# Issuing the V loads of batches 2 to 7 from GpSimd in place of the ACT queue

## The chip, the core and the metric

The kernel runs on one core of a Trainium2 chip. Its engines are TensorE (PE, matmuls), VectorE (DVE), ScalarE (ACT), GpSimd (POOL) and SyncE (SP, which here only issues transfers); 16 DMA engines move data between HBM and the on-chip memory. The metric is the device time of one execution in microseconds (us). The kernel before takes 307.86 us, the median of 3 runs (307.82 to 308.49).

## What is computed

Sliding-window causal attention over 8 batches, 8 heads, 576 positions and head size 64, followed by a two-layer network with a hard-swish:

```python
scores = (q @ k.transpose(0, 1, 3, 2)) / sqrt(64)          # 8 x 8 x 576 x 576
rel = pos[:, None] - pos[None, :]
scores = where((rel >= 0) & (rel < 64), scores, -1e9)       # window of 64
attn = softmax(scores)
x = (attn @ v).transpose(0, 2, 1, 3).reshape(4608, 512)
h = x @ w_in                                                # 512 -> 2048
y = (h * clip(h + 3, 0, 6) / 6) @ w_out                     # 2048 -> 512
```

All inputs and the output are float32 in HBM; the kernel casts to bfloat16 on chip.

## The kernel before

The program is laid out by a planner: the Python code keeps a model of when each engine is free (`pl.op(engine, ready, duration, function)`) and emits the instructions of each engine in the order that this model gives. The durations in it are only for that order; the chip runs each engine's list in order, with semaphores between engines.

Work goes in blocks of 512 rows. In block T, TensorE does the first layer (`s1`, line 812), then the second layer (`s2`, line 860), and between the matmuls of the second layer it does the scores and the PV product of batch T+1. From batch 2 on, a batch comes in through these steps:

- Q and K are loaded by SP into float32 staging tiles, cast by GpSimd into `nat`, and turned by two DMA transposes on SP (`QKT<-nat`).
- V is loaded in five pieces (four of 128 positions and a tail of 64) and cast by GpSimd twice, into `V` and, shifted by 64 positions, into `W` (which lives in a buffer that the profile names `runs`).
- Scores on TensorE (line 672), exponentials on ACT (678), mask on VectorE (683), PV on TensorE (699), division on VectorE (740), and a DMA transpose on SP into `xT`, which the next block's first layer reads.

The streaming of V, which the change touches:

```python
def stream_v(b):
    V, W = V_ring[b % 2], W_ring[b % 2]
    tiles = {}
    deps = stage_slot([...]) + (("pv", b - 2, NG - 1), ("issued", b, 1 if b == NR6 else 0))   # NR6 = 2
    tdeps = tail_slot([("cast", b, 2, KB - 1)])
    def issue(kb):                                   # kb = 0 .. 4, piece 4 is the tail
        ss = min(P, S - kb * P)
        def fn(s):
            # ... (staging tiles are taken at kb == 0)
            st = tiles["l"][:ss, :] if kb == KB - 1 else tiles["t"][:, kb, :]
            nc.scalar.dma_start(
                out=st.rearrange("p (h d) -> p h d", h=H),
                in_=v[b, :, kb * P : kb * P + ss, :].rearrange("h s d -> s h d"),
            )
            # ... (the planner's guess of when it lands)
            sv = st.rearrange("p (g h d) -> p g h d", g=NG, h=2)
            todo = [(("POOL",), W[D:P, :, kb, :, 0:D], sv[0:D], H * D)]
            if ss == P:
                todo.append((("POOL",), V[:, :, kb, :, 0:D], sv, H * D))
                todo.append((("POOL",), W[0:D, :, kb + 1, :, 0:D], sv[D:P], H * D))
            casts(("cast", b, 2, kb), land, todo)
            if kb < KB - 1:
                pl.op("ACT", s + (VGAP2 if b == NR6 else VGAP), 0.45, issue(kb + 1))   # VGAP = VGAP2 = 1.8
        return fn
    pl.op("ACT", 0.0, 0.45, issue(0), deps=deps + tdeps)
```

What waits for V: all five pieces of a batch must be cast before its first PV product.

```python
def pv(b, g):
    for r in soft(b, g) + vcasts(b, g):      # the masks, and the casts of all 5 pieces of V
        pl.wait(r)
    # ... matmuls of line 699, then reciprocal and multiplication on DVE
    def xdma(t):                              # the transpose into xT, issued by SP
        ...
        nc.sync.dma_start_transpose(out=xT[...], in_=cell["o"][...])
```

In a block the side work is placed at fixed matmuls of the second layer:

```python
REST = ((11, "S", 0), (18, "S", 1), (25, "PV", 0), (25, "PV", 1), (35, "PV", 2), (35, "PV", 3))
```

Of the kernel before, what the change touches and what calls it, by code (L numbers as in the profile page):

```python
# [24 lines left out]
VGAP = 1.8  # L25
VGAP2 = 1.8
# [79 lines left out]
def kernel(  # L106
# [9 lines left out]
    nc = tc.nc  # L116
# [19 lines left out]
    NR6 = 2  # L136
# [3 lines left out]
    pl = Plan()  # L140
# [123 lines left out]
    def stage_slot(casts):  # L264

        stage_hist.append(casts)
        return tuple(stage_hist[-1 - NSTAGE]) if len(stage_hist) > NSTAGE else ()
# [37 lines left out]
    def casts(key, land, pieces):  # L305

        left = [len(pieces)]
        def one(t):
            left[0] -= 1
            if not left[0]:  # L310
                pl.mark(key, t)
        for eng, o_ap, i_ap, cols in pieces:
            copy_op("cast", eng, cols, land, o_ap, i_ap, None, one)
# [3 lines left out]
    def tail_slot(casts):  # L317
        tail_hist.append(casts)
        return tuple(tail_hist[-4]) if len(tail_hist) > 3 else ()
# [48 lines left out]
# [4 lines that stand above are left out]
        deps = stage_slot([("cast", b, 2, i) for i in range(KB - 1)]) + (("pv", b - 2, NG - 1), ("issued", b, 1 if b == NR6 else 0))  # L372
        tdeps = tail_slot([("cast", b, 2, KB - 1)])

        def issue(kb):
            ss = min(P, S - kb * P)
            def fn(s):
                if kb == 0:
                    tiles["t"] = stage.tile([P, 4, H * D], F32, name="st", tag="st")
                    tiles["l"] = tails.tile([P, H * D], F32, name="tl", tag="tl")  # L380
                if kb == KB - 1:
                    pl.mark(("vgo", b), s)
                st = tiles["l"][:ss, :] if kb == KB - 1 else tiles["t"][:, kb, :]
                nc.scalar.dma_start(
                    out=st.rearrange("p (h d) -> p h d", h=H),
                    in_=v[b, :, kb * P : kb * P + ss, :].rearrange("h s d -> s h d"),
                )
                dma["v"] = max(dma["v"], s) + 262 * ss / P / VRATE
                land = dma["v"] + 2.7
# [4 lines that stand above are left out]
                    todo.append((("POOL",), W[0:D, :, kb + 1, :, 0:D], sv[D:P], H * D))  # L394
                casts(("cast", b, 2, kb), land, todo)
                if kb < KB - 1:
                    pl.op("ACT", s + (VGAP2 if b == NR6 else VGAP), 0.45, issue(kb + 1))
            return fn
        pl.op("ACT", 0.0, 0.45, issue(0), deps=deps + tdeps)

    def load_v_halves(b):

# [23 lines left out]
    def load_nat(b):  # L426
        for i, src in enumerate((q, k)):
# [42 lines left out]
            for kb in (KB - 1,) if i in LONG else range(KB):  # L470
                ss = min(P, S - kb * P)
                def go(s, i=i, src=src, kb=kb, ss=ss, T=T, n=n, done=done):
# [14 lines left out]
                    return fr  # L487
                yield b, deps + tail_slot([("cast", b, i, kb)]) if kb == KB - 1 else deps, go
        stream_v(b)

    WC = FF // 4
# [434 lines left out]
    for T in range(NTB):  # L926
# [3 lines left out]
        b = T + 1  # L930
# [36 lines left out]
```

The softmax here doesn't subtract the row's maximum and nothing guards it: scores larger than these inputs give would overflow.

## Time and profile before

The profile is one execution with a span of 308.0 us.

| what | before |
|---|---|
| time, median of 3 | 307.86 us |
| granted TensorE clock | 1.000 |
| DMA moved | 58.38 MB, mean 190 GB/s |
| V loads of batches 2 to 7 on the ACT queue | 24 of 256 KB, median 5.3 us from issue to landing; 6 of 128 KB, 5.9 us |
| transposes into xT | 24, median 3.4 us from issue to landing |
| transposes of Q and K | 12, median 7.6 us from issue to landing |

How to read it: busy times are sums over the span, and a busy engine is not one at its peak. In the rows of waits, "A <- B" means that A sat idle until B ended. The chain of work that ended last goes back from the last instruction to what released it, step by step, so that time on it is time that counts. A queue such as ACTq is the sequencer of an engine while it issues a transfer; the number behind it is how long the issue took, not how long the data took. A timeline row has its start, its length, the engine, the source line, the operation with the tiles it writes and reads, and in brackets the idle time before it and what ended that.

### The profile page before, as it was taken

How to read it: one execution, taken by the hardware profiler on the slowest of the kernel's cores; microseconds unless marked ns; L12 is line 12 of the kernel's file. 1: busy time of each engine (PE TensorE's matmuls, PEld its weight loads, DVE VectorE, ACT ScalarE, POOL GpSimd, SP SyncE). 2: the span in 40 equal slices, each digit the busy share in tenths (PEclk: the TensorE clock that was granted, in tenths of full speed). 3: DMA queues.
4: the chain of work that ended last, by engine and by line, in shares of the span. 5: the costliest groups of instructions: out<-in, count | busy, mean ns of one | idle time of the engine just before them, and what ended most of it. 6: DMA issues, size and time to landing. Idle time of an engine off the chain costs nothing.

```text
span 308.0 us, 6681 instructions
## 1 busy us (share of the span) xinstructions
PE 295.9 (96%) x2787; PEld 152.8 (50%) x2787; DVE 162.1 (53%) x209; ACT 154.8 (50%) x190; POOL 117.0 (38%) x185
## 2 busy tenths in 40 slices
PE   6989988999998999999999999999999999999995
PEld 2554445644543454785444554455575544444443
DVE  5576577757623755365636562656175617304610
ACT  5856586455714671467146714671367236316611
POOL 3167547618924660367127722682270000000000
PEclk9999999999999999999999999999999999999999
DMA  7999999999999996999599979997980550010011
GB/s 214 264 356 389 390 316 247 250 156 293 222 170 252 294 178 107 242 285 218 118 200 283 240 124 224 248 244 129 232 195 2 132 92 0 34 70 34 0 69 70
DMA packets 134863, 58.38 MB, mean 190 GB/s; under 512 B 117296, under 2 KB 124720, under 8 KB 134832
## 3 DMA queue, kind: packets, MB, share of 16 engines
q1 hardware_dynamic: 106560, 50.80, 72.0%
q10 hardware_dynamic: 28272, 7.15, 11.8%
q8 instruction: 22, 0.36, 0.6%
q14 instruction: 9, 0.07, 0.1%
HBM read 36.70 MB, written 9.44 MB: 150 GB/s over the span
## 4 chain that ended last, share of the span: by engine, by line
PE 71%; DMA 14%; SPq 6%; DVE 2%; POOL 2%; issue 2%; ACT 1%; ACTq 0%; POOLq 0%
PE ps L812 36%; PE acc L860 30%; DMA st<-in_moe_w_out_dram 5%; DMA xT<-opg 5%; DMA st<-in_v_dram 3%; SPq L357 2%; PE ps L672 2%; PE ps L699 2%; SPq L332 1%; DVE opg L740 1%; SPq L415 1%; ACT pT L678 1%; POOL wout L280 1%; POOL V L280 1%; SPq L747 1%
## 5 line engine op out<-in xcount | busy, mean ns | idle before, releaser
L824 DVE SCALAR_TENSOR_TENSOR gT<-t,ps 128x1024 bf16<-128x1024 bf16 x72 | 87.7, 1221 | 98.0 <-ACT t L821 98.0
L860 PE MATMUL acc<-wout,gT 128*128 128x512 bf16 (+2 forms) x592 | 132.8, 374 | 0.8 <-DVE wout L277 0.5
L812 PE MATMUL ps<-xT,win 128*128 128x512 bf16 (+4 forms) x704 | 126.6, 340 | 2.3 <-DMA xT<-opg 2.2
L821 ACT ACTIVATE t<-ps,half 128x1024 bf16<-128x1024 f32 x72 | 79.9, 1113 | 51.6 <-PE ps L812 49.6
L812 PEld LDWEIGHTS <-win 128*128 128x128 bf16 x704 | 65.1, 98 | 62.5 <-issue 2.9
L860 PEld LDWEIGHTS <-gT 128*128 128x128 bf16 x592 | 54.4, 98 | 61.7 <-issue 1.6
L878 ACT COPY osb<-acc 128x512 f32<-128x512 f32 (+2 forms) x37 | 21.4, 578 | 76.4 <-PE acc L860 69.7
L280 POOL CAST runs<-st 64x512 bf16<-64x512 f32 (+1 forms) x49 | 30.3, 619 | 72.5 <-DMA st<-in_v_dram 67.4
L280 POOL CAST nat<-st 128x512 bf16<-128x512 f32 x48 | 34.3, 734 | 11.8 <-DMA st<-in_k_dram 8.0
L678 ACT ACTIVATE pT<-ps 128x768 bf16<-128x768 f32 x36 | 26.9, 837 | 9.3 <-PE ps L672 9.3
L683 DVE TENSOR_TENSOR pT<-pT,mask 128x1152 bf16<-128x1152 bf16 x24 | 20.6, 876 | 15.9 <-ACT pT L678 15.9
L740 DVE TENSOR_TENSOR opg<-ps,rec 128x640 bf16<-128x640 f32 x32 | 26.4, 824 | 1.1
L280 POOL CAST V<-st 128x512 bf16<-128x512 f32 (+1 forms) x30 | 18.9, 632 | 4.8 <-DMA st<-in_v_dram 3.2
L622 ACT ACTIVATE pT<-ps 128x768 bf16<-128x768 f32 x16 | 12.7, 833 | 0.8 <-PE ps L613 0.7
L277 DVE CAST runs<-st 128x576 bf16<-128x576 f32 x14 | 7.9, 570 | 7.8 <-DMA st<-in_q_dram 5.7
L279 ACT COPY QKT<-ps 128x1152 bf16<-128x1152 bf16 x8 | 9.1, 1135 | 4.1 <-PE ps L582 4.1
L699 PEld LDWEIGHTS <-pT 128*64 128x64 bf16 x480 | 8.6, 111 | 5.1 <-issue 3.0
L280 POOL CAST wout<-st 128x1024 bf16<-128x1024 f32 x6 | 7.4, 1251 | 8.6 <-DMA st<-in_moe_w_out_dram 8.6
L699 PE MATMUL ps<-runs,pT 128*64 128x65 bf16 x288 | 9.9, 196 | 0.0
L672 PEld LDWEIGHTS <-QKT 64*128 64x128 bf16 x432 | 7.3, 95 | 5.1 <-issue 5.1
L699 PE MATMUL ps<-V,pT 128*64 128x65 bf16 x192 | 9.5, 197 | 0.0
L672 PE MATMUL ps<-QKT 64*128 64x64 bf16 x432 | 9.1, 194 | 0.0
(60 smaller groups left out, 117.2 us busy)
## 6 DMA issues: line engine op xcount, KB each, us to landing
out_dram<-osb SPq DMA_DIRECT2D x35, 256.0 KB, 3.9
st<-in_q_dram SPq DMA_DIRECT2D x12, 512.0 KB, 6.8
st<-in_k_dram SPq DMA_DIRECT2D x24, 256.0 KB, 6.1
st<-in_v_dram ACTq DMA_DIRECT2D x24, 256.0 KB, 5.3
st<-in_moe_w_out_dram SPq DMA_DIRECT2D x4, 1024.0 KB, 13.7
st<-in_moe_w_in_dram SPq DMA_DIRECT2D x3, 1024.0 KB, 10.2
st<-in_q_dram SPq DMA_DIRECT2D x8, 288.0 KB, 6.7
st<-in_k_dram SPq DMA_DIRECT2D x8, 288.0 KB, 7.1
```

The source lines that it names most:

```text
L280: return lambda s: nc.gpsimd.tensor_copy(out=out_ap, in_=in_ap) and None
L622: nc.scalar.activation(out=pT[:, :, kbs[0] : kbs[0] + 2, 0:QW], in_=st[:, :, 0 : 2 * QW].rearrange("p h (k w) -> p h k w", k=2), func=EXP, ...
L672: nc.tensor.matmul(st[:, h, c * D : (c + 1) * D], lhsT=kwin(b, g, i, h), rhs=turned(qk(b, 0, g), i)[h * D : (h + 1) * D], start=True, stop ...
L678: nc.scalar.activation(out=pT[:, :, part * NB * D : (part + 1) * NB * D], in_=st[:, :, 0 : NB * D], func=EXP, scale=scale,)
L683: pl.op("DVE", t, 0.8, lambda s: nc.vector.tensor_tensor(out=P_half, in0=P_half, in1=mask64[:].unsqueeze(1).unsqueeze(1).to_broadcast([P, ...
L699: nc.tensor.matmul(o[odd * D : (odd + 1) * D, h, m * VW : (m + 1) * VW], lhsT=pT[:, h, i * D : (i + 1) * D], rhs=(V if i % 2 else W)[:, g, ...
L740: nc.vector.tensor_tensor(out=opg[:].rearrange("p k h d -> p h k d"), in0=ov[:, :, :, 0:D], in1=rec[:].unsqueeze(3).to_broadcast([P, 2, KB ...
L812: nc.tensor.matmul(hs, lhsT=win16[:, g, (2 * c + j) * P : (2 * c + j + 1) * P], rhs=xs, start=(g == 0), stop=(g == NG - 1),)
L821: nc.scalar.activation(out=t1[:], in_=hT[:], func=RELU, bias=half[:], scale=1.0 / 6.0)
L824: nc.vector.scalar_tensor_tensor(out=gT[:, 2 * c : 2 * c + 2, :], in0=cell["t"][:], scalar=1.0, in1=hT[:], op0=MIN, op1=MULT,)
L860: nc.tensor.matmul(accs[ts][:, c0:c1], lhsT=gT[:, fc, ts * P : (ts + 1) * P], rhs=wout16[:, fc, c0:c1], start=(fc == 0), stop=(fc == NFC - 1),
L878: nc.scalar.copy(out=osb[:, c0:c1], in_=acc[:, c0:c1])
```

## The change

The five transfers per batch that bring V in for batches 2 to 7 are issued by GpSimd and no longer by ACT; the planner's duration for one issue goes from 0.45 to 1.0. The purpose is to free ACT, which computes the activations of the first layer and the exponentials, from issuing transfers and from the waits that these issues carry, and to have the loads issued by the engine that also casts them. What is computed stays the same.

```diff
--- before.py
+++ after.py
@@ -381,7 +381,7 @@
                 if kb == KB - 1:
                     pl.mark(("vgo", b), s)
                 st = tiles["l"][:ss, :] if kb == KB - 1 else tiles["t"][:, kb, :]
-                nc.scalar.dma_start(
+                nc.gpsimd.dma_start(
                     out=st.rearrange("p (h d) -> p h d", h=H),
                     in_=v[b, :, kb * P : kb * P + ss, :].rearrange("h s d -> s h d"),
                 )
@@ -394,9 +394,9 @@
                     todo.append((("POOL",), W[0:D, :, kb + 1, :, 0:D], sv[D:P], H * D))
                 casts(("cast", b, 2, kb), land, todo)
                 if kb < KB - 1:
-                    pl.op("ACT", s + (VGAP2 if b == NR6 else VGAP), 0.45, issue(kb + 1))
+                    pl.op("POOL", s + (VGAP2 if b == NR6 else VGAP), 1.0, issue(kb + 1))
             return fn
-        pl.op("ACT", 0.0, 0.45, issue(0), deps=deps + tdeps)
+        pl.op("POOL", 0.0, 1.0, issue(0), deps=deps + tdeps)
 
     def load_v_halves(b):
 
```

## The prediction

> **What bounds the kernel now.** I read the page's shares first, then the chain of work that ended last in order of time, then the two queues concerned as timelines.
>
> ```profile
> PE 295.9 (96%) x2787; PEld 152.8 (50%) x2787; DVE 162.1 (53%) x209; ACT 154.8 (50%) x190; POOL 117.0 (38%) x185
> PEclk9999999999999999999999999999999999999999
> DMA  7999999999999996999599979997980550010011
> ```
>
> TensorE is busy for 295.9 of 308.0 us at full clock, so all that any change elsewhere can bring is in 12.1 us, and most of that lies outside the reach of V: the first fill before 62 us and the last store. ACT is half idle, GpSimd 62% idle. The chain tells what is left:
>
> ```profile
> 60.79 13.81 PE ps L812 x64
> 79.29 0.69 PE ps L672 x36
> 79.98 1.62 PE acc L860 x7
> 81.59 0.76 PE ps L699 x40
> 87.88 5.85 DMA xT<-opg
> 93.77 13.54 PE ps L812 x62
> ```
>
> ```profile
> PE ps L812 <- DMA xT<-opg: 2.2, 2, 1.6
> ```
>
> From 60.79 us on the chain is nearly all matmuls (start, length, engine, output, line, count). The row below it, from the waits of TensorE (total, times, longest), says that from then on TensorE waits for the transposes of the attention output, 2.2 us in two places, the longer one (1.6 us) at 93.77. The windows agree: TensorE is busy 31.00 of 31.00 us in 94 to 125 and 30.88 in 125 to 156. So one block of 31 us (64 matmuls of the first layer, 13.8 us; 64 of the second with scores and PV between, 17 us) is bound by TensorE, and V does no harm as long as its casts end before the first PV (line 699) of the block: 81.59 us for batch 2, then 114.23, 145.61, 176.6, 207.6 and 239.5.
>
> When is V ready now? First the issues on the ACT queue, then the casts on GpSimd, for batch 2:
>
> ```profile
> 62.77 0.43 ACTq L384 DMA_DIRECT2D st<-in_v_dram  x1
> 64.29 0.41 ACTq L384 DMA_DIRECT2D st<-in_v_dram  x1
> 66.02 1.65 ACTq L384 DMA_DIRECT2D st<-in_v_dram  x1
> 69.55 0.38 ACTq L384 DMA_DIRECT2D st<-in_v_dram  x1
> 70.12 1.75 ACTq L384 DMA_DIRECT2D tl<-in_v_dram  x1
> ```
>
> ```profile
> 62.48 0.61 POOL L280 CAST nat<-tl 64x512 bf16<-64x512 f32 x1
> 69.37 0.62 POOL L280 CAST runs<-st 64x512 bf16<-64x512 f32 x1 [6.29 <-DMA st<-in_v_dram]
> 77.11 0.62 POOL L280 CAST runs<-st 64x512 bf16<-64x512 f32 x1
> 78.20 0.62 POOL L280 CAST runs<-tl 64x512 bf16<-64x512 f32 x1 [0.47 <-DMA tl<-in_v_dram]
> ```
>
> All five issues are out by 71.9 us, while GpSimd waits 6.29 us for the first landing and then casts as data lands. The last cast ends at 78.8, only 2.8 us ahead of PV at 81.59. The later batches have more: last casts end at 106.9, 138.5, 169.8, 201.4 and 231.4, that is 7 to 8 us ahead of PV. Batch 2 is the tight one.
>
> **What the Trainium skill says.** "DMA: Bandwidth & Descriptors", section "SWDGE vs HWDGE vs iDMA": a DMA issued from GpSimd has its descriptors computed by software on two of GpSimd's cores, one issued from SP or ACT by hardware; the page's specifications put the first byte at about 1 us against about 0.6 us. No run here shows the software side: all DMAs of the kernel before are on hardware queues. For ACT the trace has 0.38 us per issue (median 381 ns; 652 ns for the tail). The same page, "Issuing engines are not separate DMA queues": all queues end on the same 16 DMA engines, and another queue saves only issue time. The page of this kernel agrees that there is one shared resource: the DMA row above stands at 9 in most slices. "SBUF — State Buffer", section "Who interferes with whom": VectorE in its two-port modes locks GpSimd out, and with it the descriptor writing. In the steady blocks VectorE runs operations with a PSUM input, reciprocals and mask multiplications of two SBUF inputs, none of which that page lists as two-port, so I charge nothing for it.
>
> **The change, part by part.** It takes 30 issues (24 of 256 KB, 6 of 128 KB) off ACT and puts them into GpSimd's program. The built order shows TensorE, VectorE and SP with the same instructions in the same order. On GpSimd the order of a batch becomes: 10 casts of Q and K, three V issues in a row, the 3 casts of V's first piece, the fourth issue, 6 casts of pieces two and three, the tail issue, 3 casts of piece four, 1 cast of the tail.
>
> *Taken away:* 24 x 0.38 + 6 x 0.65 = 13 us of ACT's queue. ACT waits for TensorE's results in its longest rows (69.7 us and 49.6 us), so this is worth about 0 on the path. The two slow issues (1.65 and 1.75 us) delay ACT around 66 to 72 us, yet the chain shows 64 matmuls in 13.81 us there, as in quiet blocks: also 0.
>
> *Added:* g us of GpSimd per issue, five per batch. The kernel's own plan charges 1.0 (it charges 0.45 for ACT, where the trace has 0.38 to 0.65, so its numbers are near). I take g = 1.0 to 1.5 as an estimate. The profile says 28272 packets for 7.15 MB on ACT's queue, 253 bytes each: some 1,000 descriptors for each 256 KB, many for software, so I lean upwards.
>
> *Moved, and this is what I expect to cost:* issues four and five now stand behind casts in GpSimd's order. Batch 2 with g = 1.0: the casts of K end at 63.1. First issue 63.1; it took 6.5 us to land before, plus 0.6 for g against 0.4: 70.2. Three casts at 0.68 from start to start: 72.2. Fourth issue until 73.2. Six casts, 4.1: 77.3. Tail issue 77.3 to 78.3; landing 5.7 us (median before) plus 0.6: 83.6. Tail cast 0.6: 84.2. Casts of piece four lie inside that wait. With the shortest landing in the trace for these DMAs (3.2 us) it is 81.7. Against PV at 81.59 TensorE stalls 0.1 to 2.6 us, and g enters four times (first landing, fourth issue, tail issue, tail landing), so g = 1.5 adds 2.0. Middle: about 3 us, once.
>
> Does it come again? The casts of Q and K of batch 3 then start at 84.2, 10 x 0.61 and gaps: 90.7. V's chain is 84.2 - 63.1 = 21.1 us: 111.8, against PV at 114.2 + 2.6. It doesn't. GpSimd's loop is 21.1 + 6.6 = 27.7 us, under 31. With g = 1.5 it is 29.7; with g = 2 it is 31.7, over the period, and GpSimd becomes the bound. So a single loss up to g of about 1.9, and one per batch beyond.
>
> *A second move:* in later batches the first three V issues leave as soon as the K casts end, and not spaced by ACT's work. For batch 4 this was 121.0, 124.5 and 128.3; now from about 117. They take DMA time while the attention transposes (116.3 to 123.4) are in flight, on which TensorE already waits at two of the block borders. ACT's queue took 11.8% of 308 us, 36.3 us for 27 full-size equivalents: 1.35 us of all 16 engines each. One or two more of them in the way, half shared, cost 1 to 2 us at the tight borders (93.8 and about 219), less at others: +1 us in all.
>
> Sum: 307.9 + 3 + 1 = 311.9; I say 311.7.
>
> **Rivals.** *Nothing moves (307.5 to 308.5).* For it: TensorE is the bound, 2.8 to 8 us of slack before PV, issues start at once when GpSimd is free. Against it: the 2.8 us of batch 2 are less than two issues and one landing in line. It would hold if landings shorten to 3 us. *GpSimd becomes the bound (316 to 335).* For it: some 1,000 small descriptors per issue made by software; g = 2 gives 6.6 us at batch 2 and then 0.7 per batch, g = 3 some 4.7 per batch for five more. Against it: the plan's 1.0. *A gain (305.7 to 307).* For it: the free ACT queue, and V moved ahead of the QK transposes so that the attention transposes of some blocks meet less V traffic (in the block of 121.0 the first V ran right beside them). It can give back at most the 2.2 us of waits.
>
> **Range and chances.** g between 0.8 and 1.2 gives +1 to +4.5 with the transposes, 1.2 to 1.7 +4 to +7, above that more. So 308.2 to 319.0. The 2% line is 314.0, reached at g of about 1.6: I give slower 0.33, same 0.65, faster 0.02.
>
> **What would show it.** GpSimd's DMA issues should stand with about 1 us each in its queue; the last V cast of batch 2 near 84 us and TensorE waiting for it at its first PV, and no such wait later; transposes of xT landing up to 2 us later at 93 and 219 us. I am wrong if batch 2's PV doesn't wait, if the waits come back in every block (then g is above 2), or if the loss sits in the transposes and not in V.

## The result, and the profile after

The changed kernel takes 322.7 us where the kernel before takes 308.1: a ratio of 1.047 (95% interval 1.0435 to 1.0513), slower. The prediction was 311.7 us, with a range of 308.2 to 319.0. Ratios leave out executions over 1.5% above the quickest of their kernel, and so does the 322.7 us (323.3 and 322.2 are counted, 327.3 and 328.1 are not); the times of the experiments below are medians of all executions. The profiled execution has a span of 321.6 us against 308.0, 13.6 us more.

The page of the changed kernel, shares and clock, and then the queues (packets, MB, share of the 16 engines):

```profile
PE 300.0 (93%) x2787; PEld 154.6 (48%) x2787; DVE 162.1 (50%) x209; ACT 154.9 (48%) x190; POOL 138.2 (43%) x215
PEclk9999999999799999799999999999999999999999
```

```profile
q1 hardware_dynamic: 106560, 50.80, 71.7%
q0 software_dynamic: 2208, 7.08, 11.4%
```

GpSimd is busy for 138.2 us where it was 117.0, the 30 issues now among it; with 43% of the span it is far from a bound. TensorE's 4 us more are not more work, as the count of matmuls is the same: the clock row has two slices at 7. V now goes over a software queue: 2208 packets for 7.08 MB, 3.2 KB each, where the ACT queue had 253 bytes each.

What TensorE waits for after the first fill (total, times, longest), from its own waits:

```profile
PE ps L812 <- DMA xT<-opg: 9.4, 6, 2.6
PE ps L699 <- POOL runs L280: 3.1, 1, 3.1
```

The wait for xT was 2.2 us in two places and is now 9.4 in six; the wait of a PV (line 699) for a cast of V is new. The chain that ended last shows where, before and then after:

```profile
107.31 2.38 PE acc L860 x11
...
125.17 13.53 PE ps L812 x122
138.70 2.37 PE acc L860 x11
...
200.58 2.37 PE acc L860 x11
...
232.46 2.37 PE acc L860 x11
```

```profile
79.24 4.17 issue
83.45 0.61 POOL runs L280
84.10 1.09 PE ps L699 x32
85.20 3.17 PE acc L860 x10
...
110.68 2.37 PE acc L860 x11
...
123.11 8.68 DMA xT<-opg
131.83 14.96 PE ps L812 x122
146.78 2.37 PE acc L860 x11
...
189.96 8.41 DMA xT<-opg
198.41 13.54 PE ps L812 x62
211.95 2.37 PE acc L860 x11
...
225.59 6.64 DMA xT<-opg
232.27 13.37 PE ps L812 x122
245.64 2.37 PE acc L860 x11
```

I compare the ends of the first layer in each block (in the chain, the start of the group of 11 matmuls that follows): 107.31 before and 110.68 after, then 138.70 and 146.78, 169.63 and 177.72, 200.58 and 211.95, 232.46 and 245.64. So the changed kernel falls behind by 3.4, 4.7, 0.0, 3.3 and 1.8 us: once at the first PV of batch 2, and at three later borders where the chain runs through a transpose into xT. These three make 9.8 us. The border that had the longest wait before, 1.6 us at 93.77, is not among them: its wait is now 1.2 us, at 98.00.

The casts of batch 2 on GpSimd, with V's issues now among them:

```profile
62.34 2.79 POOL L384 DMA_DIRECT2D st<-in_v_dram  x3
69.16 0.62 POOL L280 CAST runs<-st 64x512 bf16<-64x512 f32 x1 [4.03 <-DMA st<-in_v_dram]
71.08 0.89 POOL L384 DMA_DIRECT2D st<-in_v_dram  x1
75.98 0.69 POOL L384 DMA_DIRECT2D tl<-in_v_dram  x1
83.43 0.62 POOL L280 CAST runs<-tl 64x512 bf16<-64x512 f32 x1 [4.19 <-DMA tl<-in_v_dram]
```

An issue takes 0.88 us (median 883 ns; 692 ns for the tail). The tail is issued at 75.98, behind nine casts, and its cast ends at 84.05; before, it was issued at 70.12 and cast by 78.8. TensorE's PV starts at 84.10, after a wait of 3.1 us. The windows around it and around two of the waits for xT show what idle time can bring with it (the length, then the busy time of TensorE, weight loads, VectorE, ACT and GpSimd, and behind the last bracket the granted clock):

```profile
80.40:84.10 3.70, 0.59 (x10) 0.23 (x9) 0.76 (x1) 0.87 (x2) 0.62 (x1) 0.93 1.14 177
84.10:88.40 4.30, 4.30 (x48) 2.19 (x49) 2.69 (x5) 0.58 (x1) 4.29 (x7) 0.66 0.74 169
128.00:131.80 3.80, 0.73 (x4) 0.19 (x2) 0.00 (x0) 0.48 (x1) 1.39 (x3) 0.94 1.02 183
131.80:136.50 4.70, 4.67 (x31) 3.54 (x31) 1.09 (x1) 1.27 (x2) 2.46 (x4) 0.68 1.21 263
194.00:198.40 4.40, 1.44 (x6) 0.49 (x5) 0.00 (x0) 0.58 (x1) 3.07 (x6) 1.00 1.15 138
198.40:203.00 4.60, 4.59 (x22) 2.11 (x22) 1.45 (x2) 2.23 (x2) 2.33 (x4) 1.00 1.21 169
```

Behind the pause the clock averages 0.66 over 4.3 us, which is worth about 1.5 us (an estimate: 0.34 of 4.3 us); ten second-layer matmuls alone take 3.17 us in the chain, where they took 2.27 before. The same follows the wait at 131.83: 122 first-layer matmuls in 14.96 us, before 13.53, so 1.4 us more. It does not follow the wait at 198.41: TensorE stood still there for 3.0 us of the window, against 3.1 us of each of the other two, and the clock stayed at 1.00. The Trainium skill, "TensorE: Matmul & The Clock Gate", section "What's actually happening", states an idle window of about 3.4 us after which the clock is halved; here two pauses of some 3 us in which few matmuls ran were enough, and a third was not.

The transfers (KB each, median us from issue to landing) show the other loss:

```profile
st<-in_v_dram POOLq DMA_DIRECT2D x24, 256.0 KB, 6.3
xT<-opg SPq DMA_TRANSPOSE x24, 5.3
QKT<-nat SPq DMA_TRANSPOSE x12, 8.7
```

The median landing of a transpose into xT goes from 3.4 to 5.3 us, and the slow ones are in the blocks that lost time: 7.6 to 8.7 us for the four ahead of the border at 131.83 (first xT issue at 119.8, V's three issues from 118.1), 4.7 to 9.1 at 198 (186.5 and 186.9), 2.6 to 9.4 at 232 (220.6 and 222.2). In the block without loss V had left 4 us ahead of the first transpose (151.4 and 155.4), and they landed in 3.6 to 5.4 us.

### The profile page after: what moved, and what is told of

Same layout as the page of the kernel before. It is cut to its first block, busy times and chain, and to the rows that moved or that the text cites. A ratio compares the mean times of both kernels' runs of the same rounds, so it can differ in the third digit from the quotient of the medians.

```text
span 321.6 us, 6689 instructions
## 1 busy us (share of the span) xinstructions
PE 300.0 (93%) x2787; PEld 154.6 (48%) x2787; DVE 162.1 (50%) x209; ACT 154.9 (48%) x190; POOL 138.2 (43%) x215
## 3 DMA queue, kind: packets, MB, share of 16 engines
q0 software_dynamic: 2208, 7.08, 11.4%
## 4 chain that ended last, share of the span: by engine, by line
PE 59%; DMA 21%; POOL 6%; SPq 6%; issue 4%; DVE 2%; ACT 1%; POOLq 0%; ACTq 0%
PE ps L812 30%; PE acc L860 24%; DMA xT<-opg 9%; DMA st<-in_v_dram 5%; DMA st<-in_moe_w_out_dram 5%; SPq L357 2%; PE ps L699 2%; POOL runs L280 2%; PE ps L672 2%; POOL V L280 1%; SPq L332 1%; DVE opg L740 1%; DMA st<-in_k_dram 1%; SPq L415 1%; ACT pT L678 1%
## 5 line engine op out<-in xcount | busy, mean ns | idle before, releaser
L812 PE MATMUL ps<-xT,win 128*128 128x512 bf16 (+4 forms) x704 | 128.8, 343 | 9.5 <-DMA xT<-opg 9.4
L812 PEld LDWEIGHTS <-win 128*128 128x128 bf16 x704 | 66.1, 99 | 71.0 <-issue 11.2
L280 POOL CAST nat<-st 128x512 bf16<-128x512 f32 x48 | 30.8, 660 | 34.8 <-DMA st<-in_q_dram 21.6
L384 POOL DMA_DIRECT2D st<-in_v_dram x24 | 21.3, 891 | 0.0
L699 PE MATMUL ps<-runs,pT 128*64 128x65 bf16 x288 | 10.5, 200 | 3.1 <-POOL runs L280 3.1
L280 POOL CAST runs<-tl 64x512 bf16<-64x512 f32 x6 | 3.7, 616 | 16.1 <-DMA tl<-in_v_dram 15.9
L737 DVE RECIPROCAL rec<-ps 128x10 f32<-128x10 f32 x32 | 6.8, 212 | 7.3 <-PE ps L699 5.5
```

The source lines that it names most:

```text
L280: return lambda s: nc.gpsimd.tensor_copy(out=out_ap, in_=in_ap) and None
L384: nc.gpsimd.dma_start(out=st.rearrange("p (h d) -> p h d", h=H), in_=v[b, :, kb * P : kb * P + ss, :].rearrange("h s d -> s h d"),)
L699: nc.tensor.matmul(o[odd * D : (odd + 1) * D, h, m * VW : (m + 1) * VW], lhsT=pT[:, h, i * D : (i + 1) * D], rhs=(V if i % 2 else W)[:, g, ...
L812: nc.tensor.matmul(hs, lhsT=win16[:, g, (2 * c + j) * P : (2 * c + j + 1) * P], rhs=xs, start=(g == 0), stop=(g == NG - 1),)
```

## The experiments

All keep TensorE's, VectorE's and SP's instructions in the same order. They are compared with the kernel before on the same chip.

### Batch 2 back on the ACT queue, and batch 2 alone on GpSimd

```diff
-                nc.gpsimd.dma_start(
+                (nc.scalar if b == NR6 else nc.gpsimd).dma_start(
```

(with the planner's engine to match; in the second kernel the condition is turned round)

> V of batch 2 goes back to the ACT queue, batches 3 to 7 stay on GpSimd. Both theories of the rest agree here: the 3.1 us that TensorE waits for the last V cast before the first PV of batch 2, and the slower clock behind that wait, go away, and the waits for the transposes into xT stay. Expected 318 to 319 us. If the wait at batch 2 were not a loss of its own (hidden in the later waits), the time would stay at 322 to 323.

> Only V of batch 2 on GpSimd, the rest on the ACT queue: the first loss alone. From the changed kernel less the run without it: 322.7 - 318.0 = 4.7 us, so 312 to 313 us, with one wait of about 3 us for the last V cast before the first PV of batch 2. If the two losses overlap, less than 310.

Measured: without batch 2 on GpSimd 318.0 us, ratio 1.034 (1.0283 to 1.0403). Batch 2 alone 312.5 us, ratio 1.018 (1.0082 to 1.0269); this ratio counts all four of its executions (309.4, 310.4, 314.7 and 315.9 us), and the lower two alone are 0.9% above the kernel before. TensorE's waits in the first and in the second:

```profile
PE ps L812 <- DMA xT<-opg: 6.5, 8, 2.5
```

```profile
PE ps L699 <- POOL runs L280: 1.7, 1, 1.7
PE ps L812 <- DMA xT<-opg: 0.7, 2, 0.4
```

The first has no wait at a PV left, the second has it and next to none for xT. So there are two losses, and they add up: 3.4% and 0.9 to 1.8% against 4.7% for both, inside the intervals. The second one's interval is wide. Its profiled execution is the quickest (309.4 us): the wait is 1.7 us there, and the clock behind it stays at 1.00, so this profile shows less than the median stands for.

### V on GpSimd, but behind the transposes

```diff
+                    if b > NR6:
+                        nc.gpsimd.tensor_copy(out=hold[:], in_=xT[:, NG - 1, x_at(b - 1) : x_at(b - 1) + 8])
                     tiles["t"] = stage.tile([P, 4, H * D], F32, name="st", tag="st")
```

(and the same dependence for the planner; the copy writes a tile that nothing reads)

> All V on GpSimd, but for batches 3 to 7 GpSimd first copies 8 elements of the last xT transpose of the batch before, so that the first V issue comes after that landing; the work added is one tiny copy per batch. If the loss is V travelling beside the xT transposes, the waits for xT fall to about 2 us in all and the time to 311 to 313 us (only the wait at batch 2 is left). If issuing from GpSimd is dear in itself (its engine time, or descriptors made by software slowing all transfers), it stays at 318 us or more.

Measured: 311.4 us, ratio 1.010 (1.0051 to 1.0149). TensorE's longest wait, and the transposes:

```profile
PE ps L702 <- POOL runs L281: 3.3, 2, 2.4
```

```profile
xT<-opg SPq DMA_TRANSPOSE x24, 2.7
```

No wait for xT is left at all (the kernel before had 2.2 us of it), and a transpose lands in 2.7 us. GpSimd issues as much as in the changed kernel, so its engine time is not what costs; V beside the transposes is. What is left is the PV of batch 2, 2.4 us, and 0.9 us at a later PV (lines are shifted by three here).

### Both together

> V of batch 2 on the ACT queue and batches 3 to 7 on GpSimd behind the landing of xT (by the tiny copy). Both losses that the theory names are then away: 306.5 to 308.5 us, with no wait for xT. If issuing from GpSimd costs something else besides, it stays above 310 us.

The edit is that of the two kernels above in one. Measured: 309.4 us, ratio 1.004 (1.0009 to 1.007). With both losses away the changed kernel is within half a per cent of the kernel before, not better, and just above the time expected. No wait for xT is left, but one for V of 1.1 us:

```profile
PE ps L702 <- POOL runs L281: 1.1, 1, 1.1
```

### Five issues in a row on GpSimd

```diff
-VGAP = 1.8
-VGAP2 = 1.8
+VGAP = 0.0
+VGAP2 = 0.0
```

> All five V issues of a batch stand in a row on GpSimd, ahead of the casts. The tail of batch 2 then lands by about 73 us, so the wait before its first PV goes (3 to 4 us less), but five loads and not three travel beside the xT transposes in the later batches: xT landings as slow as in the changed kernel or slower. Expected 318 to 324 us, with TensorE waiting 9 us or more for xT.

Measured: 330.7 us, ratio 1.074 (1.0706 to 1.0775), slower than I expected. Its profile is of its longest execution (335.9 us), so I read the places from it and not the time: TensorE waits for xT at the borders, and at batch 2 for a transpose of Q or K (line 672) for 7.0 us, which I had not expected; the wait for V behind it is still 1.8 us. To bring the tail of batch 2 forward put five loads beside those transposes, the second of which took 18.2 us to land.

### The same moment, the other queue

The early issues on the ACT queue: the kernel before, with the planner told to issue V of batches 3 to 7 when the casts of K are done.

```diff
-    deps = ... + (("pv", b - 2, NG - 1), ("issued", b, 1 if b == NR6 else 0))
+    deps = ... + (("pv", b - 2, NG - 1), ("issued", b, 1) if b == NR6 else ("cast", b, 1, KB - 1))
-VGAP = 1.8
+VGAP = 0.9
```

> V on the ACT queue as before, but for batches 3 to 7 issued as soon as the casts of K end, nearly in a row: the timing of the changed kernel with hardware descriptors. If only the timing counts, xT lands as late as in the kernel with five in a row on GpSimd (waits of 8 us or more, 316 us or more). If the queue from GpSimd takes a larger share of the DMA engines (its packets hold 3.2 KB on average, those of the ACT queue 253 bytes), the transposes suffer much less here: waits up to 4 us, 308 to 312 us.

Its counterpart has batch 2 on the ACT queue, and the others on GpSimd with a gap of 0:

> V of batch 2 on the ACT queue, batches 3 to 7 on GpSimd with all five issues in a row: the counterpart of the kernel with early issues on the ACT queue (312.6 us), the same five loads at about the same moment, on the other queue. If the queue from GpSimd takes a larger share, 318 to 323 us and waits for xT of 8 us or more. If only the timing counts, and the 330.7 us of the five in a row came from batch 2 alone, 312 to 314 us with waits of about 4 us.

Measured: on the ACT queue 312.6 us, ratio 1.016 (1.0107 to 1.0219); on GpSimd 319.8 us, ratio 1.039 (1.0344 to 1.0441). TensorE's wait for xT, ACT queue first:

```profile
PE ps L812 <- DMA xT<-opg: 4.0, 4, 2.4
```

```profile
PE ps L812 <- DMA xT<-opg: 8.2, 4, 2.8
```

So the timing alone costs 1.6% on the ACT queue, and the kernel that issues early from GpSimd costs 2.3 points more. That is not yet the queue's share, because the two do not issue at the same moment. Batch 6, ACT queue first:

```profile
177.99 2.30 ACTq L384 DMA_DIRECT2D st<-in_v_dram  x2
181.40 1.23 SPq L747 DMA_TRANSPOSE xT<-opg  x1
```

```profile
182.55 3.52 POOL L384 DMA_DIRECT2D st<-in_v_dram  x4
184.22 1.23 SPq L747 DMA_TRANSPOSE xT<-opg  x1
```

For each batch, how long V's first issue stands ahead of the first transpose into xT, and TensorE's wait for xT at the border that follows:

| us | batch 3 | batch 4 | batch 5 | batch 6 | batch 7 |
|---|---|---|---|---|---|
| ACT queue: V ahead by | 3.1 | 3.4 | 3.8 | 3.4 | 3.4 |
| ACT queue: wait | 2.9 | 0 | 0 | 0 | 1.0 |
| GpSimd: V ahead by | -2.7 | 6.0 | 2.1 | 1.7 | 4.7 |
| GpSimd: wait | 5.1 | 0 | 0 | 2.8 | 0.4 |

Of the 8.2 us that the GpSimd kernel waits, 7.9 are in batches 3 and 6, where its V leaves later against the transposes than the ACT kernel's (in batch 5 it does too, without a wait). In batch 4, where it leaves earliest, its transposes land in 3.5 to 5.0 us (4.8 to 6.5 on the ACT queue); in batch 6 in 7.1 to 9.4 us (4.2 to 6.4). The median over all is the same, 5.3 against 5.4 us. So it counts when V leaves; whether the queue itself counts is not shown.

### Rows of 2 KB on both queues

Both kernels once more, with V of batches 3 to 7 read as rows of 2 KB. What reaches V is then another arrangement of positions and heads, so the kernels leave out the right order of V; bytes, casts and matmuls stay.

```diff
-                    out=st.rearrange("p (h d) -> p h d", h=H),
-                    in_=v[b, :, kb * P : kb * P + ss, :].rearrange("h s d -> s h d"),
+                    out=st,
+                    in_=flat[kb * P * H * D : (kb * P + ss) * H * D].rearrange("(p x) -> p x", x=H * D),
```

> The early issues on the ACT queue once more, but V of batches 3 to 7 is read as rows of 2 KB and not of 256 bytes (so positions and heads come in another arrangement, and the output is not the reference's). The bytes are the same, the packets eight times larger. If the size of a packet sets the share that a queue gets, the xT transposes land later than with 256 bytes (median above 5.4 us) and the time rises from 312.6 to 315 us or more. If the loss on GpSimd's queue has to do with descriptors made by software, it stays at 312.6 or falls[...].

> The kernel with five issues in a row on GpSimd (319.8 us, batch 2 on the ACT queue), but V of batches 3 to 7 is read as rows of 2 KB, so an eighth of the descriptors for the same bytes (positions and heads come in another arrangement, the output is not the reference's). With the two early runs on the ACT queue (256 bytes 312.6 us, 2 KB 313.4 us) it makes a table of queue by row. If the harm on GpSimd's queue comes from the many descriptors that software makes, it falls to about 313 us. If it comes from how that queue shares the DMA engines whatever the descriptors, it stays at 318 to 320 us.

| ratio to the kernel before | rows of 256 bytes | rows of 2 KB |
|---|---|---|
| early, ACT queue | 1.016 (1.0107 to 1.0219) | 1.016 (1.0106 to 1.0219) |
| early, GpSimd | 1.039 (1.0344 to 1.0441) | 1.027 (1.0215 to 1.0331) |

V's queue in the page of the ACT kernel with 256 bytes, of the one with 2 KB, and of the GpSimd kernel with 2 KB (which has the same 1840 software packets with 256 bytes):

```profile
q10 hardware_dynamic: 28272, 7.15, 12.0%
```

```profile
q10 hardware_dynamic: 8112, 7.15, 8.9%
```

```profile
q0 software_dynamic: 1840, 5.90, 7.4%
```

I had thought that a queue's share goes by the size of its packets. It doesn't show: on the ACT queue the packets grow from 253 to 881 bytes on average and the time stays (313.4 us), while the transposes into xT land earlier, in a median of 4.4 us against 5.4; on GpSimd the packets stay at 3.2 KB and the time falls by 1.2 points, to 315.2 us, between the two forecasts. So that theory falls. In batches 3 and 6, where the GpSimd kernels wait, V leaves at the same moment with both kinds of row, within 0.2 us, and TensorE's wait for xT falls from 8.2 to 4.9 us in all: there the longer rows help. They change more than the number of descriptors, though: an issue takes 0.54 us and not 0.88, and a load lands in 4.6 us and not 5.5, and no run tells these apart. For the 1.1 points that are left between the queues, with intervals that nearly touch and with moments of issue that differ as above, no run here gives the cause.

### V later on the ACT queue, and a row of five later on GpSimd

```diff
-    deps = ... ("issued", b, 1 if b == NR6 else 0))
+    deps = ... ("issued", b, 1) if b == NR6 else ("s1v", b - 1))
```

> Everything on the ACT queue as in the kernel before, but the first V issue of batches 3 to 7 stands about 4 us later in ACT's order, behind the third copy of the output, so that V meets the xT transposes even less. If V beside the transposes makes the 2.2 us that TensorE waits for xT in the kernel before, that wait goes and the time is 305.5 to 307 us; if the transposes are late for another reason, 308. If V then comes too late for PV, more.

Measured: 322.4 us, ratio 1.049 (1.0437 to 1.0534). I had expected a gain. The wait for xT did go (median landing 2.7 us), but the waits of TensorE and ACT's timeline show a new one, in four batches:

```profile
PE ps L812 <- DVE gT L824: 13.1, 5, 3.2
```

```profile
134.95 1.11 ACT L821 ACTIVATE t<-ps,half 128x1024 bf16<-128x1024 f32 x1 [0.99 <-PE ps L812]
139.74 0.61 ACTq L384 DMA_DIRECT2D tl<-in_v_dram  x1
140.45 3.12 ACT L821 ACTIVATE t<-ps,half 128x1024 bf16<-128x1024 f32 x3 [4.39 <-POOL runs L280]
```

ACT sits for 4.39 us behind an issue that waits, VectorE waits for ACT's activations, and TensorE's first layer then waits 13.1 us in all for VectorE. The row names a cast, but the built program has this issue wait for the completion semaphore of the second transpose of Q and K, eight transfers back: transfers from SP and ACT take turns on eight of them, those of GpSimd have eight of their own. That transpose was issued at 130.8 and took 8.8 us: 139.6, and the issue starts at 139.74.

> The kernel with V of batches 3 to 7 on GpSimd behind the landing of xT and batch 2 on the ACT queue (309.4 us), with all five issues in a row: V is cast earlier, so the wait of 1.1 us for V at a PV should go, and the transposes of Q and K have slack to be slowed. If that holds, 306 to 308 us, under the kernel before by the 2.2 us that it waits for xT. If the five in a row slow the transposes of Q and K beyond their slack, 310 us or more with waits at the scores.

The edit is a gap of 0 in the kernel of both remedies. Measured: 317.5 us, ratio 1.030 (1.024 to 1.0361). The waits for V went, as expected, but the transposes of Q and K, which now meet V, land in 11.3 us (before 7.6), beyond their slack:

```profile
PE ps L675 <- DMA QKT<-nat: 7.7, 5, 2.3
PE ps L815 <- DMA xT<-opg: 1.6, 3, 0.9
```

So V lengthens whichever transposes it meets, and the two kinds trade. Median landings of xT and of the transposes of Q and K: 5.4 and 5.2 us with V early on the ACT queue, 3.4 and 7.6 in the kernel before, 2.7 and 8.9 with V behind xT on GpSimd, 2.7 and 11.3 with five in a row there. The kernel before lies between, and none of the others is faster.

## Why the prediction was wrong

- **TensorE is the bound, and ACT's relief is worth nothing:** right. ACT's busy time is 154.9 us (154.8), the 13 us of queue bought nothing, and every loss is TensorE waiting, or its slower clock behind a wait. With 25 of the 30 issues off ACT and V out of the way of xT, the time is still 0.4% above the kernel before.
- **The cost of an issue, 1.0 to 1.5 us:** a bit high, it is 0.88 us. GpSimd is not the bound; that rival is out. The slack that the later batches had ahead of PV was 6.2 to 8.1 us by the times given, not 7 to 8; nothing hangs on it.
- **Batch 2:** the mechanism is right; that the numbers agree nearly to the tenth is partly luck. I had the tail's issue at 77.3 and the last cast ending at 84.2; they are at 75.98 and 84.05. The issue came 1.3 us earlier than I thought and the tail's data came 7.5 us after its issue and not 6.3, and the two errors cancel. I had 3 us once; the wait is 3.1 us, and it doesn't come again at a PV, as predicted. What I didn't count is the slower clock behind it, about 1.5 us. Batch 2 alone costs 0.9 to 1.8%.
- **The second move:** here it failed. The mechanism was named: the first three V issues leave earlier and meet the transposes into xT. For batch 4 V left 4.7 us behind the first of them before, and 1.7 us ahead of it after; I had put it about 1 us behind. The step's size was off: the term "+1 us in all" measured 9.8 us at three borders in the profile (1.4 us of it the slower clock), and 3.4% (10.5 us) in the run that has batches 3 to 7 alone. I had taken V's own time on the DMA engines, 1.35 us a load, half shared, and slack at all but two borders. What the runs show instead: landings of 2.6 to 5.9 us went up to as much as 9.4, far more than half of 1.35 us for each load in the way, and two of the three borders had no wait before (125.17 and 186.76). Early loads cost 1.6% even on the ACT queue. From GpSimd they cost 3.4 to 3.9%; how much of the difference is the queue, for which I charged nothing, and how much the moment of issue, stays open. My own sign of being wrong came true: most of the loss sits in the transposes and not in V.
- **The range:** it came from g alone. The term that I sized most roughly had no spread of its own, and it was the one that moved.
- **The rival of a gain** had one thing right: with V out of the way of xT the 2.2 us of waits do go. It didn't pay: each other place for V that was tried brought a wait of its own, and no version came out under the kernel before.

## What to carry over

When a change makes transfers start earlier, list what else is in flight at that moment and whose landing the bound engine waits for; give that term a range of its own, with the landing times under load that the trace already shows and not the bytes divided by a rate. An engine that issues in order ahead of its own casts, or behind a wait, moves its issues with it: the spacing that ACT's work gave to V was part of the tuning. Test such a change by holding the issue behind the landing that it disturbs: one tiny copy separated timing from engine cost here. And before two queues are compared, line up the moments at which they issue.

## What the runs showed of the hardware

- A load of 256 KB in 256-byte rows takes GpSimd 0.88 us to issue, one of 128 KB 0.69 us; ACT needs 0.38 and 0.65 us.
- Loads of 256 KB lengthen the landing of DMA transposes that are in flight beside them: xT landed in a median of 2.7 us with V held back, 3.4 in the kernel before and 5.3 in the changed kernel (9.4 at most), the transposes of Q and K in 5.2 with V early and 11.3 with five V loads beside them. A few us matter: in one kernel and on one queue, with V 6.0 us ahead of xT it landed in 3.5 to 5.0 us, with V 1.7 us ahead in 7.1 to 9.4. That GpSimd's queue delays them more than ACT's is not shown.
- After two pauses of about 3.1 us TensorE's clock was at 0.66 and 0.68 on average over the next 4.3 and 4.7 us, which added about 1.5 us to each; after one of 3.0 us in the same trace it stayed at 1.00.
- A transfer issued from ACT can hold the activations behind it for 4.4 us, by waiting for the completion of an unrelated transpose that used the same semaphore.
